# A fused attention and MLP kernel: x fetched as fp32 and cast on chip, token sums on VectorE, other states fetched and used at other times

## The chip, the cores and the metric

One core of one Trainium2 chip. The metric is the device time of one execution in microseconds (us); smaller is better. The kernel before took 243.77 us (median of 3 runs, 243.11 to 243.97). For every run the span of the core and its mean granted TensorE clock are on record too; the clock is given as a share of full speed. Names: PE is TensorE's matmul row in the profile, PEld its weight loads, DVE is VectorE, ACT is ScalarE, POOL is GpSimd, SP is SyncE, which issues DMAs.

## The reference, cut to what matters

```python
B, H, S, Ns, D = 8, 8, 512, 32, 64          # x: (B,H,S,D), state: (B,H,Ns,D)
scores  = scale * x @ state.T               # tokens attend to 32 states
xread   = softmax(scores) @ state
scores2 = scale * state @ x.T               # states attend to 512 tokens
sread   = softmax(scores2) @ x
y = concat([xread, sread], axis=2)          # per batch 544 rows of 512
h = y @ w_in                                # 512 -> 2048
out = (h * sigmoid(h)) @ w_out              # 2048 -> 512
```

## The kernel before

Work goes batch by batch. For one batch: `scores` (a product of x transposed, `xT`, with the states transposed, `stT`), `exps` on ACT, `norm` (row sums on DVE, a multiply on POOL), a transpose of the normalised weights to `aT`, `W1` (states times `w_in`, so that xread itself is never formed), 16 first-layer products `h` (G1) with silu on ACT, and 4 x 16 second-layer products `o` (G2). The attention of batch n = b + 1 is threaded into the G2 loop of batch b. A place in that loop is written (tt, ft): token tile 0 to 3, feature tile 0 to 15. `sread` is the second attention; it needs the sum of `exp` over all 512 tokens.

How x comes in (four casting DMAs per batch, fp32 in memory, bf16 on chip, runs of 64 values) and how the other states come in:

```python
def fetch_x(b):
    x_re = x[b].rearrange("h (p c) d -> p c h d", p=128, c=4)
    for c in range(4):
        nc.gpsimd.dma_start(x_nat[b][:, c, :, :], x_re[:, c, :, :])

def load_state(q):                      # q = 0: batches 1 to 3, q = 1: batches 4 to 7
    nc.gpsimd.memset(st_f[:, q, 0:1, 0:1], 0.0)
    for i in range(1 if q == 0 else 0, 4):
        nc.sync.dma_start(st_f[ds(NS * i, NS), q], state[4 * q + i].rearrange("h n d -> n h d"))
```

The sums in `sread`, in PSUM, and what DVE does with that bank afterwards:

```python
def sread(b):
    ps = bank([128, 2, 4, 2, NS], FP32, "ps_sr")          # one of four rotating banks
    for hg in range(2):
        for c in range(4):                                  # 8 matmuls with ones
            nc.tensor.matmul(ps[:, 1, ds(2 * hg, 2), :, :], ones[:], exp_nat[b, hg][:, c, :, :],
                             start=(c == 0), stop=(c == 3), skip_group_check=True)
    # ... 16 matmuls exp x x into ps[:, 0]; reciprocal of the sums; 4 multiplies into xmT
```

Batch 0 and the steady loop, cut to the places that the change touches:

```python
w1_cols(0, [(0, 256)], (nc.scalar, nc.scalar))
load_state(0); load_state(1)
load_w_in(1024); load_w_out(8, 4); load_w_in(1536); load_w_out(12, 4)
fetch_x(1); load_x(2)
# ...
for ft in range(NFT):                   # batch 0, three token tiles at once
    if ft == 3: cast_state(0)
    if ft == 4: cast_state(1); transpose_state(0); evict_state(0, nc.vector)
    if ft == 5: transpose_state(1); evict_state(1, nc.vector)
    if ft == 3: sread(0)
# ...
if at == (0, NFT - lead):               # steady loop, n = b + 1
    scores(n, 0); scores(n, 1); exps(n, 0); exps(n, 1)
if at == (0, 14):
    for hg in range(2): norm(n, hg); transpose_a(n, hg)
if at == (1, 6):  transpose_x(n + 1)
if at == (1, 14): sread(n); load_x(n + 2)
if at == (2, 8):  w1_chunks(n, (0, 1), both)      # takes all four banks
if at == (3, 4):  w1_chunks(n, (2, 3), both)
```

The softmax here doesn't subtract the row's maximum and nothing guards it: scores larger than these inputs give would overflow.

## Time and profile before

| what | before |
|---|---|
| median time | 243.77 us |
| span of the profiled run | 240.8 us |
| PE busy | 218.7 us (91%) |
| scores of batches 1 to 7 start at | 45.07, 61.03, 84.96, 110.28, 134.68, 159.08, 183.48 us |

The starts of `scores` (timeline of PE) are the clock of this document: the difference of two of them is the length of one batch. From the scores of batch 4 on a batch takes 24.40 us; the stretch from 3 to 4 takes 25.32.

The page's busy times, and PE, granted clock and DMA in 40 slices of 6 us:

```profile
PE 218.7 (91%) x1509; PEld 104.3 (43%) x1536; DVE 77.6 (32%) x152; ACT 140.4 (58%) x235; POOL 50.0 (21%) x63
PE   7796299999999999799999999999999999999980
PEclk9769979999999999999999999999999999999997
DMA  6999992199099209910795069903810321011211
```

PE is full almost everywhere. The low slice is the fifth (24 to 30 us, digit 2). The view of the waits, for PE alone (what waited, for whom, us in total, times, longest):

```profile
PE ps_st L221 <- DVE st_b L122: 6.4, 2, 4.7
...
PE h_1201 L368 <- DMA aT<-an: 1.2, 1, 1.2
...
PE h_1523 L368 <- ACT g L389: 0.4, 1, 0.4
```

The first line is the transposes of the other states, waiting for their casts, which wait for their DMAs. The timeline of PE there (start, duration, what, and idle time before it):

```profile
22.83 0.40 PE L221 MATMUL ps_st<-ident,st_b 128*128 128x128 bf16 x4 [1.72 <-DVE st_b L122]
...
29.39 0.61 PE L221 MATMUL ps_st<-ident,st_b 128*128 128x128 bf16 x4 [4.66 <-DVE st_b L122]
29.80 1.06 PE L397 MATMUL o<-w_out_sb,g 128*128 128x512 bf16 x2
```

After the second wait two 512-column matmuls take 1.06 us; at 24.14 us, before it, two took 0.59. The clock has dropped: from 29.8 to 30.9 us it is granted at 0.50.

The chain of waits in one steady batch (start, duration, what), from sread to the first-layer products of the next batch:

```profile
115.67 0.48 PE ps_sr L309 x16
...
116.18 1.77 DVE rb L318
...
118.95 0.39 PE ps_w_1459 L342
...
121.28 0.60 ACT o_sb L120
...
121.89 1.28 ACT L389
...
123.19 1.09 ACT g L389 x2
```

Two things hold PE here. W1 (`ps_w`) needs the bank that DVE's reciprocal `rb` and four multiplies still read. Then ACT has an output copy, a table load for silu (the line at 121.89) and the first silus in a row, and `h` has only two PSUM buffers. The first of these waits stands in the full view of the waits on the row of the weight loads, about 0.6 us in each of six batches:

```profile
PEld L342 <- DVE xmT L322: 3.6, 6, 0.6
```

### The profile page before, as it was taken

To read this page: it belongs to the slowest core of one execution; us is meant where nothing else is said; L and a number is where in the kernel's file an instruction comes from. 1 tells how busy PE (TensorE), PEld (TensorE's weight loads), DVE (VectorE), ACT (ScalarE), POOL (GpSimd) and SP (SyncE) were. 2 spreads that over 40 slices of the span, in tenths; PEclk is the share of its full clock that TensorE was granted. 3 is DMA by queue.
4 is the path that set the end of the run, shared out by engine and by line. 5 is a ranking of instruction groups with operands and counts; after the bars stand their busy time and mean duration, and the time that the engine had idled before them with its cause. 6 is when DMAs were issued, how large, how long until landed. Compare 5 with 4: busy or idle time off the path is not lost.

```text
span 240.8 us, 3799 instructions
## 1 busy us (share of the span) xinstructions
PE 218.7 (91%) x1509; PEld 104.3 (43%) x1536; DVE 77.6 (32%) x152; ACT 140.4 (58%) x235; POOL 50.0 (21%) x63
## 2 busy tenths in 40 slices
PE   7796299999999999799999999999999999999980
PEld 2433133554533454344434443444344434466550
DVE  5623343660362136211821182118210831100110
ACT  2742146979649763878287827792779277644200
POOL 8581220160270027000900090003000300000000
PEclk9769979999999999999999999999999999999997
DMA  6999992199099209910795069903810321011211
GB/s 196 176 201 196 196 156 18 55 184 112 1 119 192 83 0 103 250 44 3 83 166 143 3 70 137 190 0 61 203 44 0 74 103 44 3 44 44 75 32 69
DMA packets 61149, 23.31 MB, mean 97 GB/s; under 512 B 51020, under 2 KB 56908, under 8 KB 61132
## 3 DMA queue, kind: packets, MB, share of 16 engines
q0 software_dynamic: 33888, 7.87, 37.0%
q1 hardware_dynamic: 27244, 15.21, 27.3%
q8 instruction: 12, 0.20, 0.4%
q14 instruction: 5, 0.04, 0.1%
HBM read 17.30 MB, written 8.91 MB: 109 GB/s over the span
## 4 chain that ended last, share of the span: by engine, by line
PE 64%; DMA 12%; ACT 10%; DVE 8%; issue 2%; POOL 1%; SPq 0%; ACTq 0%; POOLq 0%; DVEq 0%
PE o L397 33%; DMA w_out_sb<-in_moe_w_out_dram 6%; DVE rb L318 4%; ACT g L389 3%; DMA x_nat_237<-in_x_dram 3%; ACT L389 3%; DMA aT<-an 3%; DVE xmT L322 2%; PE ps_sc L248 2%; PE o_half L419 1%; ACT o_sb L120 1%; PE ps_sr L309 1%; PE ps_busy L128 1%; PE ps_sr L299 1%; POOL an L273 1%
## 5 line engine op out<-in xcount | busy, mean ns | idle before, releaser
L397 PE MATMUL o<-w_out_sb,g 128*128 128x512 bf16 x488 | 133.7, 382 | 1.2 <-issue 0.2
L397 PEld LDWEIGHTS <-g 128*128 128x128 bf16 x528 | 49.6, 98 | 58.6 <-issue 8.4
L273 POOL TENSOR_TENSOR an<-exp_nat,rc 128x512 bf16<-128x512 bf16 (+1 forms) x16 | 15.9, 1010 | 124.3 <-DVE rc L271 124.3
L270 DVE TENSOR_REDUCE rs<-exp_nat 128x16 f32<-128x512 bf16 x16 | 10.6, 660 | 52.3 <-ACT exp_nat L260 52.3
L120 ACT ACTIVATE o_sb<-o 128x512 f32<-128x512 f32 x15 | 8.9, 597 | 29.8 <-issue 18.4
L122 DVE COPY o_sb<-o 128x512 f32<-128x512 f32 x17 | 11.4, 669 | 46.1 <-PE o L397 46.1
L318 DVE RECIPROCAL rb<-ps_sr 128x256 f32<-128x256 f32 x8 | 14.1, 1757 | 4.3 <-PE ps_sr L309 4.3
L260 ACT ACTIVATE exp_nat<-ps_sc 128x512 bf16<-128x512 f32 x16 | 8.8, 594 | 0.9 <-PE ps_sc L248 0.8
L342 PEld LDWEIGHTS <-stT 64*32 64x32 bf16 x264 | 3.4, 89 | 13.6 <-issue 9.4
L378 PEld LDWEIGHTS <-w_in_sb 128*128 128x128 bf16 x64 | 6.3, 98 | 3.9
L260 ACT ACT_TABLE_LOAD x6 | 7.7, 1283 | 0.1
L389 ACT ACT_TABLE_LOAD x6 | 7.7, 1283 | 0.1
L322 DVE TENSOR_TENSOR xmT<-ps_sr,rb 64x64 bf16<-64x64 f32 x32 | 7.1, 222 | 0.6
L221 PE MATMUL ps_st<-ident,st_b 128*128 128x128 bf16 x8 | 1.0, 265 | 6.4 <-DVE st_b L122 6.4
L128 PE MATMUL ps_busy<-busy 128*128 128x512 bf16 x11 | 5.4, 626 | 1.5 <-DVE busy L143 1.2
L397 PE MATMUL o_a<-w_out_sb,g 128*128 128x512 bf16 x16 | 6.4, 412 | 0.0
L98 POOL DMA_DIRECT2D x_nat_237<-in_x_dram x4 | 3.5, 874 | 9.7 <-DMA w_out_sb<-in_moe_w_out_dram 4.0
L368 PEld LDWEIGHTS <-W_207 128*128 128x128 bf16 x32 | 3.2, 103 | 5.3 <-DVE W_207 L122 1.7
L299 PEld LDWEIGHTS <-ones 128*128 128x128 bf16 x64 | 4.2, 98 | 1.9
L368 PEld LDWEIGHTS <-W_1731 128*128 128x128 bf16 x32 | 3.1, 98 | 4.1 <-issue 0.8
L368 PEld LDWEIGHTS <-W_2010 128*128 128x128 bf16 x32 | 3.1, 98 | 4.1 <-issue 0.8
L368 PEld LDWEIGHTS <-W_1447 128*128 128x128 bf16 x32 | 3.1, 98 | 4.2 <-issue 0.8
(513 smaller groups left out, 350.8 us busy)
## 6 DMA issues: line engine op xcount, KB each, us to landing
out_dram<-o_sb SPq DMA_DIRECT2D x33, 256.0 KB, 3.2
w_in_sb<-in_moe_w_in_dram POOLq DMA_DIRECT2D x3, 512.0 KB, 12.3
w_out_sb<-in_moe_w_out_dram POOLq DMA_DIRECT2D x3, 512.0 KB, 14.9
x_f<-in_x_dram SPq DMA_DIRECT2D x2, 512.0 KB, 4.1
st_f<-in_state_dram SPq DMA_DIRECT2D x8, 64.0 KB, 11.8
w_in_sb<-in_moe_w_in_dram POOLq DMA_DIRECT2D x2, 256.0 KB, 8.2
w_out_sb<-in_moe_w_out_dram POOLq DMA_DIRECT2D x2, 256.0 KB, 8.7
x_nat_115<-in_x_dram POOLq DMA_DIRECT2D x4, 128.0 KB, 19.0
```

The source lines that it names most:

```text
L120: nc.scalar.activation(dst, src, func=COPY, bias=0.0)
L122: eng.tensor_copy(dst, src)
L128: nc.tensor.matmul(ps[:], busy[:, 0:128], busy[:], start=True, stop=True, skip_group_check=True)
L260: nc.scalar.activation(e[:], sc_ps[hg][:], func=EXP, bias=0.0, scale=SCALE)
L270: nc.vector.tensor_reduce(rs[:], e[:], axis=AX, op=ADD)
L273: eng.tensor_tensor(a[:, ds(c, n)], e[:, ds(c, n)], rc[:, ds(c, n)].to_broadcast([128, n, 4, NS]), op=MULT,)
L299: nc.tensor.matmul(ps[:, 1, ds(2 * hg, 2), :, :], ones[:], exp_nat[b, hg][:, c, :, :], start=(c == 0), stop=(c == 3), skip_group_check=True,)
L318: nc.vector.reciprocal(rb[:], ps[:, 1, :, :, :])
L322: nc.vector.tensor_tensor(xmT[rows, b // 4, k2, ds(32 * (b % 4), 32)], ps[rows, 0, k2, u ^ g, :], rb[rows, k2, u ^ g, :], op=MULT,)
L368: nc.tensor.matmul(ps[:], W1[b][:, hg, ds(128 * ft, 128)], aT[b][:, hg, :, :], start=(hg == 0), stop=(hg == 1), skip_group_check=True,)
L389: nc.scalar.activation(g[:, 0:n], ps[:, 0:n], func=SILU, bias=0.0)
L397: nc.tensor.matmul(outs[tt][:], gt[b * NFT + ft][:, ds(128 * tt, 128)], w_out_sb[:, ft, :], start=(ft == 0), stop=(ft == NFT - 1), skip_gr ...
```

## The change: intent and diff

x is fetched as fp32 in runs of 1 KB by one DMA and cast on chip. The other states are fetched earlier, right behind x of batch 0, and cast and transposed later. The eight sum matmuls become sums on DVE in fp32, split in two bf16 parts, and two matmuls. In the steady loop sread goes behind W1, silu's table is loaded right behind exp, and the transpose of x goes to a later place; `norm` and the transpose to `aT` move by two places, from (0, 14) to (1, 0). The core of the diff:

```diff
-    def fetch_x(b):
-        x_re = x[b].rearrange("h (p c) d -> p c h d", p=128, c=4)
-        for c in range(4):
-            nc.gpsimd.dma_start(x_nat[b][:, c, :, :], x_re[:, c, :, :])
+    x_f = pers.tile([128, H, 4, D], FP32)
     def load_x(b):
+        nc.gpsimd.dma_start(x_f[:], x[b].rearrange("h (p c) d -> p h c d", p=128, c=4))
+    def cast_x(b, eng, c0=0, nc_=4, h0=0, nh=H): ...   # eng.tensor_copy x_f -> x_nat[b]
...
-    cast_x0(1)
+    cast_x(0, nc.vector, h0=4, nh=4)
+    nc.vector.memset(st_f[:, :, 0:1, 0:1], 0.0)
+    load_state(0)
+    load_state(1)
...  # behind w1_cols(0)
-    load_state(0)
-    load_state(1)
...
-    fetch_x(1)
-    load_x(2)
+    load_x(1)
...
+    def token_sums(b):
+        f = att.tile([128, 2, 4, NS], FP32, tag="es_f", name="es_f")
+        es[b] = att.tile([128, 2, 2, 4, NS], BF16, tag="es", name="es")
+        for hg in range(2):
+            nc.vector.tensor_reduce(f[:, hg], exp_nat[b, hg].rearrange("p c s n -> p s n c"), axis=AX, op=ADD)
+        nc.vector.tensor_copy(es[b][:, 0], f[:])
+        nc.vector.tensor_tensor(es[b][:, 1], f[:], es[b][:, 0], op=SUB)
...  # sread: two matmuls with ones over es[b] instead of eight over exp_nat
...  # batch 0
-        if ft == 3: cast_state(0)
-        if ft == 4: cast_state(1); transpose_state(0); evict_state(0, nc.vector)
-        if ft == 5: transpose_state(1); evict_state(1, nc.vector)
-        if ft == 3: sread(0)
+        if ft == 1: token_sums(0)
+        if ft == 4: sread(0)
+        if ft == 5: cast_state(0)
+        if ft == 6: transpose_state(0); evict_state(0, nc.vector); cast_state(1)
+        if ft == 9: transpose_state(1); evict_state(1, nc.vector)
+        if ft == 12: cast_x(1, nc.vector); load_x(2)
...  # last token tile of batch 0
         if ft == 11: pe_transpose_a(1, 0, nc.scalar); pe_transpose_a(1, 1, nc.vector)
+            for c in range(4): cast_x(2, nc.gpsimd, c, 1)
+            load_x(3)
             transpose_x(2)
+        if ft == 4: token_sums(1)
         if ft == 13: sread(1)
...  # steady loop
                     scores(n, 0); scores(n, 1); exps(n, 0); exps(n, 1)
+                    nc.scalar.activation(warm[:], warm[:], func=SILU, bias=0.0)
-                if at == (0, 14):
+                if at == (1, 0):
                     # norm, transpose_a
+                    # cast_x(n + 1) on GpSimd in four pieces; load_x(n + 2)
+                if at == (1, 8): token_sums(n)
-                if at == (1, 6): transpose_x(n + 1)
+                if at == (3, 8): transpose_x(n + 1)
-                if at == (1, 14): sread(n); load_x(n + 2)
+                if at == (3, 10): sread(n)
```

(Statements are put on one line here; the effect is the same.)

More of the change, by code (lines that the diff above doesn't have):

```diff
@@ L13 @@
 MULT = mybir.AluOpType.mult
+SUB = mybir.AluOpType.subtract
 EXP = mybir.ActivationFunctionType.Exp
@@ L90, with cast_x @@
     xT = {}
-    def new_x(b):
-        x_nat[b] = xpool.tile([128, 4, H, D], BF16, tag="x_nat", name=f"x_nat{b}")
-    def fetch_x(b):
-        x_re = x[b].rearrange("h (p c) d -> p c h d", p=128, c=4)
-        for c in range(4):
-            nc.gpsimd.dma_start(x_nat[b][:, c, :, :], x_re[:, c, :, :])
-    def load_x(b):
-        new_x(b)
-        fetch_x(b)
+    x_f = pers.tile([128, H, 4, D], FP32)
+    def load_x(b):
+        nc.gpsimd.dma_start(x_f[:], x[b].rearrange("h (p c) d -> p h c d", p=128, c=4))
+    def cast_x(b, eng, c0=0, nc_=4, h0=0, nh=H):
+        if b not in x_nat:
+            x_nat[b] = xpool.tile([128, 4, H, D], BF16, tag="x_nat", name=f"x_nat{b}")
+        eng.tensor_copy(
+            x_nat[b][:, ds(c0, nc_), ds(h0, nh), :],
+            x_f[:, ds(h0, nh), ds(c0, nc_), :].rearrange("p h c d -> p c h d"),
+        )
     def transpose_x(b):
@@ L130, in keep_busy @@
             )
-    x_f = pers.tile([128, 8, 4, D], FP32)
     warm = pers.tile([128, 1], FP32)
@@ L148 @@
     nc.gpsimd.memset(st_f[0:NS, 0], 0.0)
-    new_x(0)
-    new_x(1)
     load_w_in(0, 256)
@@ L191, in pe_transpose_x @@
             copy(engs[u], xT[b][:, ds(m * u, m), ds(2 * hg, 2), :], ps[:])
-    def cast_x0(hg):
-        copy(
-            nc.vector,
-            x_nat[0][:, :, ds(4 * hg, 4), :],
-            x_f[:, ds(4 * hg, 4), :, :].rearrange("p h c d -> p c h d"),
-        )
-    cast_x0(0)
+    cast_x(0, nc.vector, h0=0, nh=4)
     pe_transpose_x(0, 0, 2, lambda sh, dt, nm: psO.tile(sh, dt, tag="o", name=nm))
-    cast_x0(1)
+    cast_x(0, nc.vector, h0=4, nh=4)
+    nc.vector.memset(st_f[:, :, 0:1, 0:1], 0.0)
     def load_state(q):
-        nc.gpsimd.memset(st_f[:, q, 0:1, 0:1], 0.0)
         for i in range(1 if q == 0 else 0, 4):
@@ L291, in pe_transpose_a @@
         copy(eng, aT[b][:, hg, :, :], ps[:])
+    es = {}
+    def token_sums(b):
+        f = att.tile([128, 2, 4, NS], FP32, tag="es_f", name="es_f")
+        es[b] = att.tile([128, 2, 2, 4, NS], BF16, tag="es", name="es")
+        for hg in range(2):
+            nc.vector.tensor_reduce(
+                f[:, hg], exp_nat[b, hg].rearrange("p c s n -> p s n c"), axis=AX, op=ADD
+            )
+        nc.vector.tensor_copy(es[b][:, 0], f[:])
+        nc.vector.tensor_tensor(es[b][:, 1], f[:], es[b][:, 0], op=SUB)
     def sread(b):
         ps = bank([128, 2, 4, 2, NS], FP32, "ps_sr")
-        for hg in range(2):
-            for c in range(4):
-                nc.tensor.matmul(
-                    ps[:, 1, ds(2 * hg, 2), :, :],
-                    ones[:],
-                    exp_nat[b, hg][:, c, :, :],
-                    start=(c == 0),
-                    stop=(c == 3),
-                    skip_group_check=True,
-                )
+        for part in range(2):
+            nc.tensor.matmul(
+                ps[:, 1, :, :, :],
+                ones[:],
+                es[b][:, part],
+                start=(part == 0),
+                stop=(part == 1),
+                skip_group_check=True,
+            )
         for kt in range(4):
@@ L472 @@
             ready = sum(W0[ft]) // 128
-        if ft == 3:
+        if ft == 1:
+            token_sums(0)
+        if ft == 4:
+            sread(0)
+        if ft == 5:
             cast_state(0)
-        if ft == 4:
-            cast_state(1)
+        if ft == 6:
             transpose_state(0)
             evict_state(0, nc.vector)
-        if ft == 5:
+            cast_state(1)
+        if ft == 9:
             transpose_state(1)
             evict_state(1, nc.vector)
-        if ft == 3:
-            sread(0)
+        if ft == 12:
+            cast_x(1, nc.vector)
+            load_x(2)
         if ft in (7, 11, 12):
@@ L514 @@
             pe_transpose_a(1, 1, nc.vector)
+            for c in range(4):
+                cast_x(2, nc.gpsimd, c, 1)
+            load_x(3)
             transpose_x(2)
+        if ft == 4:
+            token_sums(1)
         if ft == 13:
             sread(1)
-            load_x(3)
         if ft >= 14:
@@ L542 @@
                             transpose_a(n, hg)
-                    if at == (1, 6):
+                        if n + 1 < B:
+                            for c in range(4):
+                                cast_x(n + 1, nc.gpsimd, c, 1)
+                        if n + 2 < B:
+                            load_x(n + 2)
+                    if at == (1, 8):
+                        token_sums(n)
+                    if at == (3, 8):
                         if n + 1 < B:
                             transpose_x(n + 1)
-                    if at == (1, 14):
+                    if at == (3, 10):
                         sread(n)
-                        if n + 2 < B:
-                            load_x(n + 2)
                     if at == (2, 8):
```

## The prediction

> **What bounds the kernel now.** TensorE: 91% busy of a 240.8 us span (busy table), but three places lose time.
>
> 1. Batch 0. In the TensorE timeline it waits 1.72 us (21.1 to 22.8) and 4.66 us (24.7 to 29.4) for the casts of the fetched states (the waits view: 6.4 us, ps_st on st_b). The state DMAs go out at 11.6 to 15.9 and take a median 11.8 us to land, because they share the DMA engines with the weights, which stream at about 200 GB/s until 32.6 us (issue plus landing of the last w_out load). Afterwards the clock is at 0.5 until 32.5.
> 2. Each steady batch. The chain of waits, 115 to 126 us: sread's matmuls end, DVE reciprocal 1.76 us and four multiplies 0.93 us hold a PSUM bank that W1 needs (about 0.35 to 0.5 us stall at 118.5); later a table load of 1.28 us sits on ScalarE before the first silu and holds h (0.36 us wait, then about 0.2 us more). The period of scores is 24.4 us.
> 3. Batch 3. aT lands 6.15 us after its issue because the x fetch (256-byte source runs, DMA share 3.5) runs beside it; TensorE idles about 1.5 us near 96.5.
>
> **What the change does.**
> States are issued at about 7.3 us (after the second cast of x of batch 0), so they land before the casts at ft 5 and 6 need them. Removes the 6.4 us wait and the cold clock. The next limit is the weight stream (total bytes unchanged): w_out of ft 12 still at about 32.6 us. x of batch 1 comes behind it as fp32 in 1 KB runs. The first x load ran so at 357 to 379 GB/s (3 to 5 us), the casting ones at 154 GB/s; the Trainium skill (DMA: Bandwidth & Descriptors, Specifications) states that runs under 512 B lose line rate, and this trace agrees. So 1 MB needs about 2.8 us: landed at 35.5 to 36; DVE cast 1.23 us (estimate from 0.70 us for half); transposes of x of batch 1 at about 37.2 instead of 42.9. Gain 5.5 us; TensorE will idle a little on weights and on this x.
>
> Token sums: 8 matmuls of 128 columns (0.45 us in the chain) become 2 of 256 (0.22 us, estimate): 0.23 us per batch, on TensorE's path. New DVE work about 2.1 us per batch (two reduces near 0.68 us, a copy, a subtract), hidden: DVE is 32% busy.
>
> sread moves away from W1, and the silu table is loaded right after exp: removes the stalls of point 2, about 0.8 us per batch. Point 3's stall goes too, as the fetch now starts after the GpSimd casts (about 0.75 us each, 3 us per batch; Trainium skill, GPSIMD Engine Reference, section 3.1: 769 ns for 512 elements; no cast in this trace, a two-input multiply of that size took 1.05 us). GpSimd is 21% busy: hidden.
>
> DMA transpose of x now starts about 9.5 us before scores; alone it took about 5 us (168 to 173), so it fits.
>
> Sum: 5.5 + 6 batches at 1.0 + 1.3 (point 3) = 12.8 us; I take off about 1 us for new waits.
>
> **Prediction: 232 us, range 228 to 237. Faster by over 2%: 0.94; within 2%: 0.04; slower: 0.02.**
>
> **Right if:** no ps_st wait on st_b; transposes of x of batch 1 near 37 us, waiting for x or its cast; scores 23.3 us apart; no aT wait at batch 3; casts on GpSimd under 1 us each. **Wrong if:** early states delay the weights more than they save (waits on w_in or w_out above 3 us), x of batch 1 lands past 38 us, GpSimd casts take over 1.5 us and transposes of x then stall scores, or DVE's added sums delay W1 evictions.

## The result, and the profile after

The changed kernel took 230.17 us (median of 4 runs, 229.03 to 230.57) beside 243.87 us for the kernel before (4 runs). The ratio is 0.9428, 95% interval 0.938 to 0.9477. Here and below a ratio is the mean time of one kernel's fast runs over that of the kernel before in the same rounds, so not quite the ratio of the medians that are quoted.

The page after:

```profile
PE 213.5 (94%) x1462; PEld 102.4 (45%) x1488; DVE 103.2 (45%) x186; ACT 142.5 (62%) x241; POOL 45.8 (20%) x64
PE   7799899799999999999999999999999999999970
PEclk9999999999999999999999999999999999999997
DMA  6999974585169115911591159113611311111111
```

The low fifth slice is gone. A small one is left, the eighth (40 to 46 us, digit 7). The waits of PE:

```profile
PE ps_sr L307 <- DVE es L299: 1.2, 1, 1.2
PE ps_st L217 <- DVE st_b L124: 0.8, 1, 0.8
...
PE ps_sr L307 <- DVE es L300: 0.5, 1, 0.5
```

The wait of `ps_st` fell from 6.4 to 0.8 us, and those on `aT` and on silu (`ACT g`) are gone. The new line is sread of batch 1 waiting for the DVE sums. The timeline of PE shows it (and explains the eighth slice): PE does nothing useful between 43.6 and 45.6 us except one matmul.

```profile
43.24 0.38 PE L405 MATMUL o<-w_out_sb,g 128*128 128x512 bf16 x1
44.83 0.28 PE L307 MATMUL ps_sr<-es,ones 128*128 128x256 bf16 x1 [1.21 <-DVE es L299]
45.57 0.27 PE L307 MATMUL ps_sr<-es,ones 128*128 128x256 bf16 x1 [0.45 <-DVE es L300]
```

The chain of a steady batch is now all PE, from W1 over the first-layer products to sread, whose sums take 0.22 us where they took 0.45:

```profile
110.18 2.05 PE o L405 x9
112.23 0.43 PE h_1458 L376 x2
...
116.99 0.22 PE ps_sr L307 x2
117.21 0.47 PE ps_sr L317 x16
```

Where the time came from, by the starts of `scores` in the two traces:

| stretch | before | after | difference |
|---|---|---|---|
| start to scores of batch 1 | 45.07 | 38.97 | -6.10 |
| scores of 1 to 2 | 15.96 | 17.51 | +1.55 |
| 2 to 3 | 23.93 | 22.80 | -1.13 |
| 3 to 4 (the aT wait before) | 25.32 | 23.24 | -2.08 |
| 4 to 7 | 73.20 | 69.71 | -3.49 |
| 7 to the end | 57.32 | 56.07 | -1.25 |
| span | 240.8 | 228.3 | -12.50 |

So about half is won in batch 0, half in steps of 1.16 us (24.40 less 23.24) in the steady batches, and 1.55 us are given back in batch 1. (The spans are printed to 0.1 us, so the last stretch is known no better.)

### The profile page after: what moved, and what is told of

Same layout as the page of the kernel before. It is cut to its first block, busy times and chain, and to the rows that moved or that the text cites. A ratio compares the mean times of both kernels' runs of the same rounds, so it can differ in the third digit from the quotient of the medians.

```text
span 228.3 us, 3733 instructions
## 1 busy us (share of the span) xinstructions
PE 213.5 (94%) x1462; PEld 102.4 (45%) x1488; DVE 103.2 (45%) x186; ACT 142.5 (62%) x241; POOL 45.8 (20%) x64
## 3 DMA queue, kind: packets, MB, share of 16 engines
q0 software_dynamic: 6672, 11.54, 22.6%
## 4 chain that ended last, share of the span: by engine, by line
PE 88%; DVE 6%; issue 1%; ACT 1%; POOL 0%; POOLq 0%
PE o L405 46%; PE ps_sc L244 2%; PE ps_sr L317 2%; PE o_half L427 2%; PE ps_xt L185 1%; PE ps_busy L130 1%; PE o_a L405 1%; DVE rs L266 1%; DVE es_f L296 1%; PE ps_sr L307 1%; DVE rb L326 1%; DVE W_214 L124 1%; ACT exp_nat L256 1%; ACT xT_143 L122 1%; DVE x_nat_141 L101 0%
## 5 line engine op out<-in xcount | busy, mean ns | idle before, releaser
L405 PE MATMUL o<-w_out_sb,g 128*128 128x512 bf16 x489 | 132.1, 380 | 0.5
L124 DVE COPY o_sb<-o 128x512 f32<-128x512 f32 x17 | 11.8, 692 | 64.4 <-PE o L405 64.1
L296 DVE TENSOR_REDUCE es_f<-exp_nat 128x128 f32<-128x512 bf16 x16 | 15.3, 1000 | 0.0
L96 POOL DMA_DIRECT2D x_f<-in_x_dram x7 | 6.5, 924 | 20.6 <-DVE x_nat_486 L101 19.1
L256 ACT ACT_TABLE_LOAD x6 | 7.7, 1283 | 0.1
L553 ACT ACT_TABLE_LOAD x6 | 7.7, 1283 | 0.1
L350 PEld LDWEIGHTS <-stT 64*32 64x32 bf16 x264 | 2.8, 89 | 9.1 <-issue 8.5
L405 PE MATMUL o_a<-w_out_sb,g 128*128 128x512 bf16 x15 | 5.8, 396 | 0.1
L376 PEld LDWEIGHTS <-W_214 128*128 128x128 bf16 x32 | 3.2, 106 | 5.1 <-DVE W_214 L124 1.5
L300 DVE TENSOR_TENSOR es<-es_f,es 128x256 bf16<-128x256 f32 x8 | 5.1, 638 | 0.3
L376 PEld LDWEIGHTS <-W_400 128*128 128x128 bf16 x32 | 3.1, 98 | 3.9 <-issue 0.3
L307 PE MATMUL ps_sr<-es,ones 128*128 128x256 bf16 x16 | 3.2, 273 | 1.7 <-DVE es L299 1.2
L376 PEld LDWEIGHTS <-W_1420 128*128 128x128 bf16 x32 | 3.1, 98 | 3.6 <-issue 0.2
```

The costliest lines, as they stand in the source:

```text
L124: eng.tensor_copy(dst, src)
L256: nc.scalar.activation(e[:], sc_ps[hg][:], func=EXP, bias=0.0, scale=SCALE)
L296: nc.vector.tensor_reduce(f[:, hg], exp_nat[b, hg].rearrange("p c s n -> p s n c"), axis=AX, op=ADD)
L376: nc.tensor.matmul(ps[:], W1[b][:, hg, ds(128 * ft, 128)], aT[b][:, hg, :, :], start=(hg == 0), stop=(hg == 1), skip_group_check=True,)
L405: nc.tensor.matmul(outs[tt][:], gt[b * NFT + ft][:, ds(128 * tt, 128)], w_out_sb[:, ft, :], start=(ft == 0), stop=(ft == NFT - 1), skip_gr ...
L553: nc.scalar.activation(warm[:], warm[:], func=SILU, bias=0.0)
```

## The experiments

All twelve runs computed the right result. Runs e1 to e3 start from the kernel before, the others from the changed kernel. Three calls were made (e1, e2, e3, e7; e0, e4, e5, e6; e8 to e11); each ran on another chip and has its own runs of the kernel before, at a median of 243.4 to 243.9 us, so runs of different calls are compared by their ratios. A run counts as slow when it is more than 1.5% above the fastest of its kernel; the ratios leave slow runs out, the medians don't. Slow runs were seen in e6 (three of six) and e7 (two of four) alone.

| run | what | median us | ratio to before (95%) | period of scores, us |
|---|---|---|---|---|
| e0 | changed kernel again | 229.26 | 0.9414 (0.9375 to 0.9453) | 23.24 |
| e1 | before, states used later | 237.11 | 0.9717 (0.967 to 0.9764) | 24.40 |
| e2 | before, states fetched earlier | 239.17 | 0.9806 (0.9746 to 0.9866) | 24.40 |
| e3 | before, both | 234.81 | 0.9628 (0.9586 to 0.9669) | 24.40 |
| e4 | changed, eight sum matmuls | 229.40 | 0.9433 (0.9394 to 0.9472) | 23.46 |
| e5 | changed, silu table loaded late | 231.94 | 0.9522 (0.9483 to 0.9561) | 23.66 |
| e6 | changed, sread at the old place | 255.58 | 1.0408 (1.0347 to 1.0469) | 26.9 to 27.7 |
| e7 | changed, casting x fetch | 236.83 | 0.9623 (0.9553 to 0.9693) | 24.3 and more |
| e8 | changed, sums of batch 1 later | 227.59 | 0.9358 (0.933 to 0.9386) | 23.23 |
| e9 | e4 and sread at the old place | 231.86 | 0.9535 (0.9508 to 0.9562) | 23.97 |
| e10 | casting x fetch, issued later | 229.32 | 0.9409 (0.9381 to 0.9437) | 23.24 |
| e11 | eight sum matmuls in batches 0 and 1 | 228.75 | 0.9403 (0.9372 to 0.9433) | 23.24 |

### e0: the changed kernel beside e4 to e6

No edit.

> The changed kernel again, for comparison with the others of this call: 230 us, period of scores 23.24 us.

229.26 us, period 23.24: as before.

### e1, e2, e3: which half of the state change removes the wait?

The change does two things to the other states: the DMAs go out about 3.7 us earlier (7.9 instead of 11.6 us), and the casts and transposes stand later in the program. The prediction credited the first. e1 does only the second, e2 only the first, e3 both.

```diff
# e1
-        if ft == 3: cast_state(0)
-        if ft == 4: cast_state(1); transpose_state(0); evict_state(0, nc.vector)
-        if ft == 5: transpose_state(1); evict_state(1, nc.vector)
+        if ft == 5: cast_state(0)
+        if ft == 6: transpose_state(0); evict_state(0, nc.vector); cast_state(1)
+        if ft == 9: transpose_state(1); evict_state(1, nc.vector)
# e2
-    load_state(0); load_state(1)            # behind w1_cols(0)
+    nc.vector.memset(st_f[:, :, 0:1, 0:1], 0.0); load_state(0); load_state(1)   # behind cast_x0(1)
```

> The kernel before, states fetched as late as ever (11.6 us), but cast and transposed later (casts at ft 5 and 6, transposes at ft 6 and 9, as in the changed kernel). Theory P (as predicted): the early fetch removes the 6.4 us wait; then this run keeps at least 4 us of ps_st wait and stays at 242 us or more. Rival Q: the states landed at about 22.3 and 28.7 us in the trace of before, and TensorE would reach ft 6 at about 24.5 and ft 9 at about 29 us, so later use alone is enough: ps_st wait at most 1.5 us, transposes of x of batch 1 at 37 to 38.5 us, about 238.5 us.

> The kernel before, states fetched early (behind x of batch 0, about 7.5 us), but cast and transposed at the old places (ft 3 to 5). Theory P: ps_st wait at most 1 us, about 238 us. Rival Q: the states now land at about 17 and 24 us, while TensorE reaches ft 4 at 21 and ft 5 at about 22.5 us, so a ps_st wait of 1.5 to 3 us is left and the time is 239.5 to 241.5 us.

> The kernel before with both: early fetch and later use. Both theories: ps_st wait at most 1 us. P: same as e2. Q: same as e1 within 1 us. About 238 us, which would be 5.5 to 6 us of the 13.7 us gained; a rest of this size, 8 us, must then come from the steady batches.

e1 took 237.11 us, e2 239.17, e3 234.81, beside 243.92. The timeline of PE for the state transposes, first e1, then e2:

```profile
24.36 0.40 PE L221 MATMUL ps_st<-ident,st_b 128*128 128x128 bf16 x4
29.59 0.40 PE L221 MATMUL ps_st<-ident,st_b 128*128 128x128 bf16 x4 [1.13 <-DVE st_b L122]
```

```profile
22.13 0.39 PE L224 MATMUL ps_st<-ident,st_b 128*128 128x128 bf16 x4
25.11 0.40 PE L224 MATMUL ps_st<-ident,st_b 128*128 128x128 bf16 x4 [1.08 <-DVE st_b L122]
```

Each half alone brings the wait of 6.4 us down to 1.1. Theory P (only the early fetch counts) falls: with the fetch as late as ever, later use alone gains 6.8 us. Rival Q holds in direction; e2's time lies in its range to within 0.4 us, though its wait of 1.1 us is smaller than the 1.5 to 3 that Q put there. (The profiled run of e2 was the fastest of its four, 237.54 us, so the wait in the others isn't known.) Together they gain 9.1 us, less than the sum of the two (6.8 and 4.75), because both remove the same wait. That is more than the 5.5 us that the prediction had for batch 0 and more than the changed kernel shows there (6.10 in its trace).

A caution about sizes: the first 17 us scatter. In the trace of e3 a pair of 512-column matmuls took 0.59 to 0.60 us from 13.9 us on, in that of the changed kernel 1.06 us at 14.4 us. Five traces are of one and the same program up to the scores of batch 1 (the changed kernel, e0, e5, e6, e8): its first second-layer product starts between 13.90 us (e8) and 15.69 us (the changed kernel), and these scores between 37.10 us (e8) and 39.00 us (e0). So single traces of batch 0 differ by up to 1.9 us without any cause in the program, and the 6.10 us is one draw of 6.1 to 8.0.

### e4: the sums back on TensorE

```diff
-        for part in range(2):           # ones x es[b][:, part]
+        for hg in range(2):
+            for c in range(4):          # ones x exp_nat[b, hg][:, c]
-            token_sums(...)             # all three places
```

> The changed kernel with the token sums taken back to eight matmuls with ones (no sums on DVE). Theory P: TensorE loses 0.23 us per batch in 7 or 8 batches, plus 1.6 to 1.9 us, so 231.7 us. Rival S: the trace of the change shows TensorE idle for about 2 us near 44 us, waiting for the DVE sums of batch 1, which this kernel doesn't have; then the two cancel and the time is within 0.5 us of the changed kernel.

229.40 us, the same as e0. The period is 23.46, so 0.22 us per batch are lost to the eight matmuls, and the predicted 0.23 holds. It is given back in batch 1: scores of batch 1 to those of batch 2 take 15.96 us here, 17.52 in e0. This trace also had one aT wait of 0.9 us, and its batch 0 was 0.8 us shorter, which is within the scatter. Rival S stands: as placed, the DVE sums pay nothing in total.

### e5: the silu table late

```diff
                     exps(n, 1)
-                    nc.scalar.activation(warm[:], warm[:], func=SILU, bias=0.0)
```

> The changed kernel without the silu table load right behind exp in the steady batches: the load (1.28 us) stands again before the first silu. Theory P: the period of scores grows by 0.4 to 0.6 us, 232.5 to 233.5 us. Rival T: with sread and its DVE work moved away the load has room, growth under 0.15 us per batch, under 231 us.

231.94 us; period 23.66, so 0.42 us per batch, as theory P had it. (The time is a little under P's range, which was reckoned from 230 us for e0.) The timeline of ACT shows what stands in the way; each `L397` behind it is silu:

```profile
111.72 0.60 ACT L122 ACTIVATE o_sb<-o 128x512 f32<-128x512 f32 x1 [0.95 <-ACT W L122]
112.33 1.28 ACT L397 ACT_TABLE_LOAD   x1
113.63 1.08 ACT L397 ACTIVATE g<-h 128x512 bf16<-128x512 f32 x2
```

The same load costs nothing 6 us earlier, behind exp, where ACT has nothing else to do.

### e6 and e9: sread at its old place

```diff
-                    if at == (3, 10):
+                    if at == (1, 14):
                         sread(n)
```

> The changed kernel with sread back at its old place in the steady batches (second token tile, ft 14), ahead of W1. Theory P: W1 waits for the PSUM bank that the reciprocal and the multiplies hold, period of scores longer by 0.35 to 0.5 us, 232.2 to 233.2 us. Rival U: no wait, under 231 us. DVE is also fuller there now (sums of 2.1 us and more just before), so a growth above 0.5 us would mean that the sums add to it.

255.58 us, slower than the kernel before; the three runs that count as fast took 252.13 to 254.28 us, and the trace is of one of them. Neither theory had this, only the last sentence of the expectation. The waits of PE say why:

```profile
PE ps_sr L307 <- DVE es L299: 15.2, 7, 2.8
PE ps_sr L307 <- DVE es L300: 2.7, 7, 0.5
```

At (1, 14) the DVE sums of the batch aren't ready. So sums on DVE and the later sread belong together, and e6 says nothing of the bank. e9 takes the sums off DVE as well and is read against e4:

> The changed kernel with eight matmul sums and sread at its old place (second token tile, ft 14); to be read against e4 (eight sums, sread late; period 23.46 us). Theory P: the old place alone costs 0.35 to 0.5 us per batch through the PSUM bank: period 23.8 to 23.95 us, 231.5 to 232.5 us. Rival U: the old place costs nothing by itself and the 26.9 us period of e6 was the wait for the DVE sums alone: period 23.5 us, 229.5 us.

231.86 us, period 23.97 against 23.46 in e4: the old place costs 0.51 us per batch by itself, and theory P stands. The waits of PE alone don't name it, the full view does, on the row of the weight loads of W1; it is the wait of the kernel before, and the traces of e4 and of the changed kernel don't have it:

```profile
PEld L351 <- DVE xmT L331: 3.7, 6, 0.6
```

In the timeline of PE the 16 matmuls of the first W1 group, ten matmuls behind sread, take 1.13 us to get through, and 0.62 us in the trace of e4, where sread stands elsewhere; the difference is the 0.51:

```profile
106.41 0.63 PE L318 MATMUL ps_sr<-exp_nat,x_nat 128*128 128x64 bf16 x16
106.87 2.32 PE L406 MATMUL o<-w_out_sb,g 128*128 128x512 bf16 x9
109.12 1.13 PE L351 MATMUL ps_w<-w_in_sb,stT 64*32 64x512 bf16 x16
```

The three steady parts, 0.22 (sums), 0.51 (sread behind W1) and 0.42 (table), add up to 1.15 us; measured from before to after are 1.16. The periods also form a chain: 24.40 (before), 23.97 (e9), 23.46 (e4), 23.24 (e0). The first step, 0.43, is the table's 0.42 and leaves nothing for the moves that no run tests alone (`norm`, the two transposes, the fp32 fetch) in a batch that nothing disturbs.

### e7 and e10: is it the form of the x fetch, or its time?

e7 fetches x of batches 1 to 7 as before, with casting DMAs, at the program places where the changed kernel loads fp32. e10 does the same, but issues the fetch behind sread.

```diff
# e7
     def load_x(b):
-        nc.gpsimd.dma_start(x_f[:], ...)
+        for c in range(4):
+            nc.gpsimd.dma_start(x_nat[b][:, c, :, :], x_re[:, c, :, :])
-            cast_x(...)                  # batches 1 to 7; xpool gets three buffers
# e10: as e7 with two buffers, and
-                        if n + 2 < B: load_x(n + 2)      # behind norm at (1, 0)
                     if at == (3, 10):
                         sread(n)
+                        if n + 2 < B: load_x(n + 2)      # and load_x(3) behind sread(1)
```

> The changed kernel, but x of batches 1 to 7 fetched as before by four casting DMAs straight into x_nat (three buffers), at the places where the changed kernel loads x; no casts on GpSimd or DVE for them. Theory P: fp32 fetch is worth about 1.3 us (the aT wait of one batch) plus up to 1 us at batch 1: 231 to 232.5 us. Rival R: most of the gain in the steady batches comes from taking the 256-byte casting fetches off the DMA engines: period of scores back to 24 us or more, 235 us or more.

> As e7 (x fetched by four casting DMAs, no casts on chip), but issued behind sread of the batch (two buffers), so that they start some 8 us later, when aT has landed. Theory P (format): the 256-byte fetch itself costs, waits go on elsewhere (transposes of x late, ps_sc waits): 232 us or more. Rival V (timing): e7 was slow only because the fetch ran beside the transposes of aT; moved off them it costs nothing: no aT waits, period 23.25 us, 229 to 230.5 us.

e7 took 236.83 us with a large scatter: two of its four runs were 233.64 and 235.59 us, the other two (238.07 and 238.56, one of them the profiled one) lie more than 1.5% above the fastest and count as slow. The ratio uses the first two alone and is still 5 us worse than e0. Its trace, which is of a run counted as slow, names the wait, and in that trace the period is 24.3 to 24.6 us and once 29.5, but 23.24 in the one steady batch that fetches no x:

```profile
PE h L379 <- DMA aT<-an: 6.8, 4, 3.3
```

The line of the timeline in the batch of 29.5 us:

```profile
116.79 0.59 PE L379 MATMUL h<-aT,W 128*128 128x512 bf16 x1 [3.35 <-DMA aT<-an]
```

Behind this wait the granted clock was 0.50 from 118 to 122 us. If all four batches that fetch took 24.3 to 24.6, that would be 4 to 5.5 us (an estimate from this trace), and the fast runs lose 5.

e10 took 229.32 us: period 23.24, no aT wait, the same as the changed kernel. Yet its software DMA queue takes as much as before. The queue line of the page, packets, MB and share of 16 engines' span, first e10, then the changed kernel:

```profile
q0 software_dynamic: 33888, 7.87, 37.1%
```

```profile
q0 software_dynamic: 6672, 11.54, 22.6%
```

So rival V stands. The fp32 fetch relieves the DMA engines, and this buys no time. What matters in these runs is that no casting fetch of x runs beside the transposes of aT; the changed kernel keeps its fetch off them by putting the casts ahead of the next fetch, e10 by waiting for sread. An fp32 fetch issued as early as that of e7 was not run. Nor is the fetch the only thing that can delay an aT: in the trace of e11 PE waits 0.8 us for that of batch 7, when no x is left to fetch. What delayed that one is open. The expected 231 to 232.5 us for e7 were too low, and so was the value that the prediction gave to an undisturbed aT.

### e8 and e11: the wait of batch 1

```diff
# e8
-        if ft == 4:  token_sums(1)
-        if ft == 13: sread(1)
+        # behind transpose_x(2) at ft 11:
+            token_sums(1)
+                if b == 1 and at == (0, 6): sread(1)     # in the loop of batch 1
# e11
     # sread(b): eight matmuls if b < 2, else two; no token_sums(0), no token_sums(1)
```

> The changed kernel with one repair: the DVE sums of batch 1 are issued behind the last copy of aT of batch 1, and sread of batch 1 goes into the loop of batch 1 (first token tile, ft 6), so TensorE need not wait for them. If the 1.66 us wait of ps_sr on es near 44 us, and the aT copy held behind the sums, are the cost: 1.5 to 2 us faster than the changed kernel, 227.3 to 227.9 us. If another wait takes its place: no gain, 229 us.

> The changed kernel with eight matmul sums for batches 0 and 1 and DVE sums only from batch 2 on. The sums of batch 0 seem to hold the W1 evictions on DVE by about 1 us, those of batch 1 cost 1.66 us of waiting, and the matmuls of two batches cost 0.46 us: 1.5 to 2.3 us faster than the changed kernel, 227 to 228 us. If the cost of batch 0 is only scatter of the start: 1 to 1.5 us faster.

e8 took 227.59 us, 1.7 us less than e0's median and inside the expected range. Its ratio is 0.9358 against 0.9414 (e0; the intervals just overlap). Its trace shows the cause cleanly: scores of 1 to 2 take 16.00 us where the changed kernel takes 17.51, and no `ps_sr` wait is left; the line of the timeline where sread of batch 1 now stands shows no wait before it:

```profile
48.37 0.38 PE L307 MATMUL ps_sr<-es,ones 128*128 128x256 bf16 x2
```

This is the fastest of the kernels run.

e11 took 228.75 us, 0.5 us less than e0 and less than expected. Its period and its 15.96 us from scores 1 to 2 are as wanted, but its batch 0 is no shorter (transposes of x of batch 1 at 36.17 us) and shows 2.3 us of waits on `w_in`. That the DVE sums of batch 0 cost a microsecond is therefore not shown, and the kept traces speak against it: from the first second-layer product to the scores of batch 1, where these sums are made, it takes 22.73 to 23.85 us in the five traces with them (the changed kernel, e0, e5, e6, e8) and 22.65 and 23.31 us in e9 and e4, which have none.

## Why the prediction was right

The measured 230.17 us lies in the predicted range (228 to 237, around 232), and nearly every step showed up, but not every cause was the right one. In the traces the parts are 6.10 us in batch 0, six steady steps of 1.16 us and 0.92 us for the aT wait, less 1.55 us in batch 1: 12.4 us. Predicted were 5.5, six of 1.0 and 1.3, less 1: 11.8 us. Two of these agreements are partly luck: the 6.10 is one draw of 6.1 to 8.0, and the 1 us taken off stood for no wait that the prediction named.

- *State wait and batch 0, gain 5.5 us.* Measured 6.10 to the scores of batch 1; the transposes of x of batch 1 began at 36.78 us (predicted 37.2), the `ps_st` wait fell to 0.8. A rest of the wait that was to vanish stayed, and the transposes waited for nothing, where the prediction had them wait for x or its cast. The cause was only half seen: the prediction names the later places ("the casts at ft 5 and 6") but credits the early fetch alone, and e1 shows that the later use alone gains 6.8 us, more than the early fetch alone (4.75). Both together gain 9.1.
- *The weight stream as the next limit.* Not seen in the trace of the change: no wait on `w_in`, `w_out` or on x of batch 1 is listed. The largest landing times put the last weights at 30.8 us or earlier and x of batch 1 at 33.6, not 32.6 and 35.5 to 36. PE's own work was the limit. (e10 and e11 do show 2.3 us of waits on `w_in`, so it is near.)
- *Token sums, 0.23 us per batch.* 0.22 by e4. The DVE work was mis-sized: a reduce takes 1.00 us, not 0.68. "Hidden" holds for the steady batches and fails in batch 1, where sread followed too soon: 1.55 us came back. The prediction set 1 us aside for new waits without naming this one. Taken over the kernel, the sums pay nothing until e8 moves them.
- *sread and table, 0.8 us per batch.* 0.51 by e9 and 0.42 by e5, 0.93 together.
- *The aT wait of batch 3, 1.3 us.* 0.92 came back there (2.08 less 1.16). The cause (the x fetch beside it) is right, and so is the reason given for its going: the fetch "now starts after the GpSimd casts". e7 shows that with the new order and an early casting fetch it would have cost far more, and e10 that the time of the fetch is enough: with the casting form kept, nothing is lost.
- *x faster as fp32.* The comparison of 357 to 379 with 154 GB/s was between written fp32 and written bf16. 154 GB/s written are 308 GB/s read (an estimate, twice as many bytes), so the rate does fall, but by far less than it looks: the same x takes 3.4 us at 154 (0.524 MB), 2.8 to 2.9 us at 357 to 379 (1.05 MB). No time hung on it.
- *GpSimd casts 0.75 us, hidden.* 0.60 to 0.80 us, mean 0.62 to 0.67, hidden. The transposes of x landed in time: no `ps_sc` wait in the steady batches.
- *Scores 23.3 us apart.* 23.24.

## What to carry to other kernels

A wait on a DMA that lands late has two cures, to fetch earlier and to use later, and the second costs one moved line; test each alone before crediting the one in the title. When work moves from the bottleneck to an idle engine, check every place where the result is needed soon after: the gain of seven batches was lost in the one where the consumer stood too near. A transfer that is in nobody's way needn't be made cheaper; keep it away from the short transfers that somebody waits for.

## What the Trainium skill lacked or had wrong

- "DMA: Bandwidth & Descriptors", Specifications, says that transfers under 512 B lose line rate. The traces agree for the load on the engines (queue share 37.1% with the casting fetch of e10, 22.6% with fp32; no run separates the short runs from the cast), but the page gives no help in judging whether that is time: e10 and the changed kernel (e0) take 229.32 and 229.26 us. No page has a time for the case that hurt, a short DMA transpose beside a bulk fetch: landing of aT 6.15 us in the disturbed batch before, a median of 2.4 us in e10.
- "ScalarE: Activation LUTs", What ACT_TABLE_LOAD costs, gives about 1283 ns for the load and about 1380 ns of drain more, 2.66 us in total. The load took 1.28 us here, but the next silu began 0.02 us behind it (113.63 after a load from 112.33), so 1.3 us in total.
- "TensorE: Matmul & The Clock Gate", Seeing it yourself (HAM trace caveats), says that clock events in a trace can be unreliable. In the trace of the change the granted clock reads 1.00 from 10 to 15 us, while two 512-column matmuls at 14.36 us took 1.06 us, as long as the two before the change at 29.80 us, where the granted clock reads 0.50 (29.8 to 30.9 us). Here the length of a matmul was the better sign.
- "GPSIMD Engine Reference", section 3.1, measured 769 ns for 512 elements in a loop that it calls the best case; the fp32 to bf16 cast of 512 elements took 0.60 to 0.80 us, so it can be faster than that. Its Key points say that GpSimd shares SBUF interfaces with VectorE; no page has a size for this pair: the DVE copy of the sums took 0.29 us at 18.15 us, where GpSimd ran nothing, and 0.70 us at 132.35 us, beside GpSimd casts. That the sharing is the cause is not tested.
- "VectorE: DVE Perf Modes", The perf-mode tier table, has `tensor_reduce` at its 1× mode, with no word on strides or the number of outputs. With 512 inputs and 16 outputs it took 0.66 us, with 512 inputs in strides and 128 outputs 1.00 us; no run here separates the two.
